# Filter ticks of a fused FFT convolution and spectral mix, moved from ticks 0 to 16 of the first pair to ticks 1 to 17

## The chip, the core and the metric

The kernel runs on one core of one Trainium2 chip. A core has TensorE (matmuls), VectorE and ScalarE (both read PSUM and copy or combine tiles), GpSimdE and SyncE; here the last two mostly issue DMAs. Each engine works through its own list of instructions in order, and semaphores hold an instruction until what it needs is there. The metric is the device time in microseconds (us) of one execution, as the median of several; less is better. The profile calls the engines PE, PEld (TensorE's weight loads), DVE, ACT, POOL and SP; SPq is SyncE's DMA queue.

## The reference: a causal convolution and a spectral mix

Two steps follow each other, on `x` of 8 x 5696 x 128 (batch, positions, channels):

```python
L = 2 * S
y = np.fft.irfft(np.fft.rfft(x, n=L, axis=1) * np.fft.rfft(h, n=L, axis=0)[None], n=L, axis=1)[:, :S]
x = y
X = np.fft.rfft(x, axis=1)                      # 64 lowest modes are mixed by w_r + i w_i
Yr = einsum("bmd,mde->bme", Xr, w_r) - einsum("bmd,mde->bme", Xi, w_i)
Yi = einsum("bmd,mde->bme", Xr, w_i) + einsum("bmd,mde->bme", Xi, w_r)
u = x + np.fft.irfft(Y, n=S, axis=1)
out = u + np.maximum(u @ w_ch, 0.0)
```

The long FFT is done as matrix products: 5696 is 89 x 64, a transform over the 89 is the first stage, one over the 64 with its twiddle factors the second, and the product with the transformed filter `h` stands between the way forward and the way back.

## The kernel before

**Pairs and ticks.** The eight batches are worked through as four pairs. A pair has 90 frequencies of the first stage, in 23 *ticks* of four (the last has two). The function `tick` (line 664) puts on record what belongs to one tick, engine by engine; each engine runs its list in the order of recording, and the recorder adds the waits (a write to a PSUM bank waits until the engines that read it are done). For tick t of the first pair it records, in this order:

- in ticks 3, 5, 7, 9, 11, 14, 17 and 20 a *placement* (`x_place`, line 364): VectorE copies a piece of the next pair's input from where it was loaded to `Xin`;
- the *second stage* of tick t (`second`, line 609): 16 matmuls of tile As with the strip M into two PSUM banks. `slot_of` (line 602) says which: banks 0 and 1 in the ticks that have a filter tick and in every odd tick, and 2 and 3 in even ticks without one;
- the *product* with the filter (`products`, line 629): ScalarE copies the two banks to a tile Xs (`copied`, line 589), and VectorE multiplies it with the filter's tiles Hs to U (line 652);
- the first step of the way back for tick t-2: four matmuls of U with Wc, ScalarE's two copies to Zs, and one DMA on SyncE that stores them to DRAM (`zscr<-Zs`);
- the *modes* of tick t-3: matmuls of G with Zs, summed in bank 7;
- a *filter tick* (`filter_tick`, line 490): the transform of `h` for one tick's frequencies.

Tick 0 is different: its second stage stands ahead of the loop but for its last eight columns, and its product is made of two pieces on VectorE (line 623), between which ScalarE copies bank 7 to Xs.

**The filter tick.** `filter_tick(f, banks)` makes 16 matmuls of Ah with M (eight in the last, f = 22), one copy of the two banks to Hs, and two DMAs on SyncE that put the same columns into the other half of Hs with the two halves of the partitions exchanged (`Hs<-Hs`). Product f needs the copy and both DMAs. For odd f up to 11 a DMA for a piece of the table G follows. The copy is made by ScalarE for f below 8 (but for f = 2) and by VectorE after that; the condition is in line 506. Filter ticks 0 to 5 stand among the first pair's first stage (tile As), and 6 to 22 in its ticks, always in banks 2 and 3. LH is 6, NT is 23, and the condition for a tick of the first pair to have one is in `with_h_at`, line 584:

```python
    def with_h_at(g_, t):
        return g_ == 0 and t + LH < NT
...
            return XSLOT[(t + 1) % 2 if not with_h_at(g_, t) else 0]
...
        if with_h:
            filter_tick(t + LH, [2, 3])
```

So filter tick t + 6 stands at the end of tick t, for t from 0 to 16. The eight semaphores of the ring for `Hs<-Hs` let four filter ticks be under way.

**Around the pair.** The first stage of the next pair (As) stands at the pair's end, copied by VectorE and ScalarE in turn. Later pairs have no filter ticks. The mix of the modes and the way back with the outputs follow after the four pairs.

Of the kernel before, what the change touches and what calls it, by code (L numbers as in the profile page):

```python
# [123 lines left out]
def bass_long_conv_fft__then__afno_spectral_mix_kernel(nc, x, h, moe_w_r, moe_w_i, moe_w_ch, out):  # L124
# [10 lines left out]
    NT = (NK + KT - 1) // KT  # L135
# [149 lines left out]
    def ap(t, row, p0, n, off, dims):  # L285
        return bass.AP(t, p0 * row + off, [[row, n]] + [list(d) for d in dims])
# [5 lines left out]
    def pv(bank, off, dims, p0=0, n=P):  # L292
        return bass.AP(ps, p0 * 4096 + bank * 512 + off, [[4096, n]] + [list(d) for d in dims])
# [5 lines left out]
    def bank(i):  # L299
        return ("bank", i)  # L300
# [3 lines left out]
    def evac(dst, src, reads, writes, scale=None, eng=None, after=()):  # L304
        e = eng
        if e is None:
            turn[0] ^= 1
            e = "scalar" if turn[0] else "vector"
        if e == "scalar":
            if scale is None:  # L310
                R.add(e, lambda h_: h_.copy(dst, src), reads, writes, after=after)  # L311
            else:
                R.add(e, lambda h_: h_.activation(dst, src, COPY, scale=scale), reads, writes, after=after)  # L313
        elif scale is None:
            R.add(e, lambda h_: h_.tensor_copy(dst, src), reads, writes, after=after)  # L315
        else:
            R.add(e, lambda h_: h_.tensor_scalar_mul(dst, src, scale), reads, writes, after=after)  # L317

    def dma(eng, dst, src, ring, reads=(), writes=(), after=()):
        R.add(eng, lambda h_: h_.dma_start(dst, src), reads, writes, ring=ring, after=after)  # L320

    def mm(o, l, r, st, sp, reads, writes):
        R.add("tensor", lambda h_: h_.matmul(o, l, r, start=st, stop=sp), reads, writes)  # L323
# [3 lines left out]
    def once(key, toks):  # L327
        if key in first:
            return []
        first[key] = 1  # L330
        return list(toks)
# [3 lines left out]
    def turns(name, items):  # L335
        i = ring2.get(name, 0)
        ring2[name] = i + 1
        return items[i % len(items)]
# [25 lines left out]
    def x_place(i, src, toks):  # L364
        R.add("vector", lambda e: e.tensor_copy(bass.AP(x_sb, i * XN * XS, [[XW, NQ], [XS, XN], [1, D]]),  # L365
                                                src),
              list(toks) + XZ, [("xin", i)])
# [51 lines left out]
    def mtok(k):  # L419
        t = [("m", k // KP)]  # L420
        if k % KP == KP - 1 and k < NK - 1:
            t.append(("m", k // KP + 1))
        return t
# [17 lines left out]
    for j in range(16):  # L441
        t = turns("h", [0, 2, 4])
# [7 lines left out]
        for i in range(LONG if j == 15 else 0):  # L450
# [5 lines left out]
             eng="vector" if j in (3, 7) else "scalar")  # L456
# [25 lines left out]
    def xtok(n):  # L482
        return [("xt", n, p_) for p_ in range(2)]

    def x_room(g_, i):
        if g_ > 1:
            return x_st[i]
        return x_h[i] if i < NXH else x_st[i - NXH]

    def filter_tick(t, banks):  # L490
        n = len(ticks[t])
        hb = banks
        for i, k in enumerate(ticks[t]):
            for r in range(2):
                for dh in range(2):
                    mm(pv(hb[dh], i * DH, [[1, DH]]),
                       ap(m_sb, MW, J * dh, J, k * 3 * J + (J if r == 0 else 0) + dh * J, [[1, P]]),
                       ap(ah_sb, HW, J * dh, J, (2 * k + r) * DH, [[1, DH]]), r == 0, r == 1,
                       AHT + mtok(k) + [("ag", k)], [bank(hb[dh])])
        lo, hi = KT * t * D, (KT * t + n) * D  # L500
        old = once("xr", [t_ for r_ in XR for t_ in r_]) if t == 0 else []
        for i in range(NXH):
            if KT * t + n > KH[i // 2]:
                old = old + once(("xh", i), xtok(i))
        evac(h_sb[:, lo:hi], pv(hb[0], 0, [[DH, n], [512, 2], [1, DH]]), [bank(hb[0]), bank(hb[1])], [("h", t, 0)],
             eng="scalar" if t < LH + 2 and t != 2 else "vector",
             after=old)
        for p0, p1 in ((0, J), (J, 0)):
            dma("sync", h_sb[p0:p0 + J, HW + lo:HW + hi], h_sb[p1:p1 + J, lo:hi], "s", [("h", t, 0)], [("h", t, 1, p0)])
        if t % 2 and t // 2 < NG:  # L510
            s0, s1 = t // 2 * GP, min(t // 2 * GP + GP, NS)
            dma("sync", g_sb[:, s0 * P:s1 * P], bass.AP(c_g, s0 * P, [[GW, P], [1, (s1 - s0) * P]]), "c", (),
                [("g", t // 2)], after=[("ag", k) for k in range(s0, s1)])
# [66 lines left out]
    LC, LM, LH = 2, 3, 6  # L580
# [1 line left out]
    XBANKS = [bank(0), bank(1), bank(2), bank(3)]  # L582

    def with_h_at(g_, t):
        return g_ == 0 and t + LH < NT

    onchip = {}

# [7 lines left out]
    def twin(g_, t):  # L596
        return g_ > 0 and t % 2 == 1

    def straight(g_, t):
        return g_ > 0 and t % 4 == 3  # L600
# [8 lines left out]
    def second(g_, t, d0=0, d1=D, bs=(0, 1)):  # L609
        sl = slot_of(g_, t)  # L610
        rd = AST if d1 == D else [("as", j) for j in range(d1 // 4)]
        for i, k in enumerate(ticks[t]):
            for r in range(2):
                for b in bs:
                    col = k * 3 * J + (J if r == 0 else 0) + b * J
                    mm(pv(sl + b, i * D + d0, [[1, d1 - d0]]),
                       ap(m_sb, MW, J * b, J, col, [[1, P]]),
                       ap(a_sb, AW, J * b, J, (2 * k + r) * D + d0, [[1, d1 - d0]]), r == 0, r == 1,
                       rd + mtok(k), [bank(sl + b)])
# [44 lines left out]
    def tick(g_, t):  # L664
        if g_ + 1 < NP:
            for i in range(2 * XC):
                if t == XPLACE[g_ > 0][i]:
                    x_place(i, bass.AP(x_room(g_ + 1, i), 0, [[XB, NQ], [D, XN], [1, D]]), xtok(i))
        with_h = with_h_at(g_, t)
        if t < NT:  # L670
            of_two = t > 0 and twin(g_, t - 1)
            if not of_two:
                if straight(g_, t):
                    second(g_, t + 1)
                if t:
                    second(g_, t)
                if t == 1:
                    d_ = DA if g_ else DF
                    second(g_, 0, d_, D, (0,))
                    first_u(0, (ps, slot_of(g_, 0) * 512), 4096, bank(slot_of(g_, 0)), d_, D)  # L680
            products(g_, t, slot_of(g_, t))
            if straight(g_, t):
                copied(g_, t + 1, slot_of(g_, t + 1))
            elif twin(g_, t):
                second(g_, t + 1)
        if g_ + 1 < NP:
            i = t // 2 - 1 if t % 2 == 0 else -1
            if g_ == 0:
                i = XLATE.index(t) + NXH if t in XLATE else -1
            if 0 <= i < 2 * XC:  # L690
                x_load(g_ + 1, i, x_room(g_ + 1, i), xtok(i), [("u", t % NU)] + AST)
        if LC <= t < NT + LC:
            s_ = t - LC
            n = len(ticks[s_])
            i, zi = s_ % NU, zroom(g_, s_)
            zb = [turns("z", ZBANK) for b in range(2)]
            for b in range(2):
                for r in range(2):
                    mm(pv(zb[b], 0, [[1, n * D]]), (W1, W2)[r], u_s[i][:, r * 1024 + b * 512:r * 1024 + b * 512 + n * D],
                       r == 0, r == 1, [("u", i), ("wc",)], [bank(zb[b])])  # L700
                evac(bass.AP(z_s[zi], b * D, [[1024, P], [2 * D, n], [1, D]]),
                     pv(zb[b], 0, [[D, n], [1, D]]), [bank(zb[b])], [("zs", zi, b)], eng="scalar",
                     after=once(("zx", zi, b), Z_OLD) if zi >= NZ else ())
                if b == 0:
                    drained(g_, t, 0)
            zo = (g_ * NK + KT * s_) * P * 256
            dma("sync", bass.AP(zs, zo, [[256, P], [P * 256, n], [1, 256]]),
                bass.AP(z_s[zi], 0, [[1024, P], [256, n], [1, 256]]), "z",
                [("zs", zi, 0), ("zs", zi, 1)], [("zd", g_, s_)])
        drained(g_, t, 1)  # L710
        late = g_ + 1 < NP and t in (NT, NT + 1)
        if late and t > NT:
            modes(g_, t - LM - 1)
            drained(g_, t, 2)
        if LM <= t < NT + LM and not (late and t == NT):
            modes(g_, t - LM)
        if with_h:
            filter_tick(t + LH, [2, 3])

    def drained(g_, t, at_):  # L720
        if g_ + 1 < NP:
# [244 lines left out]
```

## Time and profile before

| | |
|---|---|
| median of 3 runs | 372.16 us (371.73 to 372.21) |
| the profiled execution's own time | 371.89 us |
| its span, first to last instruction | 370.1 us |
| TensorE busy (share of the span), instructions | 354.7 us (96%), 5350 |
| VectorE | 291.8 us (79%), 332 |
| ScalarE | 316.2 us (85%), 499 |
| GpSimdE | 75.2 us (20%), 117 |
| granted TensorE clock, mean | 0.999 |
| DMA | 103.94 MB, mean 281 GB/s |

The page gives busy times of the engines and shares of the span. A line of the timeline has the start in us from the span's start, the time in us, the engine, the line of the kernel, the operation, and the tiles as out<-in with their shapes; what stands in brackets at the end is how long the engine was idle before it, and what it waited for. L311 and L315 are the copies of one helper (ScalarE and VectorE), L323 is the helper of all matmuls and L320 of all DMAs, so the tiles tell one use from another: `ps<-As,M` is the second stage, `ps<-Ah,M` a filter tick, `ps<-U,Wc` the way back, `ps<-G,Zs` the modes. The first pair's ticks run from about 42 to 88 us of the span. The chain of waits follows the work back from the last instruction to what released it. For DMAs a view by tile gives the time from issue to landing. A table by stretches of time gives the busy times, the granted clock and the share in which the DMA engines were busy (it can be a little over 1).

### The profile page before, as it was taken

Reading aid. Unit: us, or ns where it says so; the run is one execution under the profiler, and the core shown is the slowest. Engines: PE = TensorE matmul, PEld = TensorE weight load, DVE = VectorE, ACT = ScalarE, POOL = GpSimd, SP = SyncE. Lnnn points to the kernel's source line nnn. Section 1 sums busy time; section 2 is a strip of 40 time slices with the busy share of each in tenths; the row PEclk is TensorE's granted clock in tenths of the full one; section 3 lists DMA queues with packets and bytes.
Section 4 is the critical chain, followed back from the end, with each engine's and each line's share of the span. In section 5 each row is a group of like instructions: output and inputs, shape, how many; then the busy total and the mean of one; then the engine's idle time right before and its main releaser. Section 6 shows DMA issues by size and latency. Waiting matters only on the chain.

```text
span 370.1 us, 12455 instructions
## 1 busy us (share of the span) xinstructions
PE 354.7 (96%) x5350; PEld 276.5 (75%) x5350; DVE 291.8 (79%) x332; ACT 316.2 (85%) x499; POOL 75.2 (20%) x117
## 2 busy tenths in 40 slices
PE   7999899999999999999999999999999999999994
PEld 7878766667866668866668766668899888888873
DVE  3549899988999999989999988775357777756666
ACT  8559999999999999999999999995467777688885
POOL 8804012100833311823213001151000000000000
PEclk9999999999999999999999999999999999999999
DMA  7999979969999996999996999999999999999878
GB/s 139 209 271 382 249 165 292 232 198 283 93 140 213 263 258 186 132 160 215 263 278 128 171 310 363 342 345 388 381 410 386 413 410 408 418 399 376 326 291 349
DMA packets 87048, 103.94 MB, mean 281 GB/s; under 512 B 22730, under 2 KB 72522, under 8 KB 83438
## 3 DMA queue, kind: packets, MB, share of 16 engines
q1 hardware_dynamic: 64610, 81.33, 62.5%
q0 software_dynamic: 22384, 21.83, 35.4%
q8 instruction: 42, 0.69, 0.7%
q14 instruction: 12, 0.10, 0.1%
HBM read 70.61 MB, written 51.12 MB: 329 GB/s over the span
## 4 chain that ended last, share of the span: by engine, by line
PE 78%; ACT 10%; DMA 7%; DVE 3%; issue 1%; POOL 1%; DVEq 0%; POOLq 0%
PE ps L323 78%; ACT As L313 6%; DMA out_dram<-O 5%; DMA Hin<-in_h_dram 2%; ACT R L898 1%; DVE As L317 1%; ACT Xs L311 1%; DVE U L623 1%; POOL Hin L320 1%; ACT UT L311 1%; DVE O L899 0%; ACT Zs L311 0%; DVE Hp L438 0%; ACT C L313 0%; DVE Hs L315 0%
## 5 line engine op out<-in xcount | busy, mean ns | idle before, releaser
L652 DVE TENSOR_TENSOR U<-Xs,Hs 128x2048 f16<-128x2048 f16 (+1 forms) x72 | 85.8, 1197 | 12.1 <-ACT Xs L311 11.5
L323 PE MATMUL ps<-U,Wc 128*128 128x512 f16 (+1 forms) x368 | 93.8, 376 | 1.4 <-DVE U L623 1.4
L311 ACT CAST Xs<-ps 128x1024 f16<-128x1024 f32 (+1 forms) x76 | 75.0, 995 | 5.8 <-PE ps L323 3.1
L311 ACT CAST Zs<-ps 128x512 f16<-128x512 f32 (+1 forms) x132 | 70.1, 605 | 0.7
L899 DVE TENSOR_TENSOR O<-ps,R 128x512 f32<-128x512 f32 x81 | 52.4, 684 | 21.6 <-ACT R L898 11.4
L898 ACT ACTIVATE R<-ps 128x512 f32<-128x512 f32 (+1 forms) x92 | 50.5, 592 | 8.5 <-PE ps L323 8.4
L317 DVE TENSOR_SCALAR As<-ps 128x720 f16<-128x720 f32 x64 | 53.1, 879 | 4.8 <-PE ps L323 3.3
L323 PE MATMUL ps<-As,M 64*128 64x128 f16 (+3 forms) x1504 | 52.5, 214 | 2.4 <-ACT As L313 1.2
L313 ACT ACTIVATE As<-ps 128x720 f16<-128x720 f32 (+1 forms) x68 | 48.2, 771 | 5.0 <-PE ps L323 4.8
L323 PE MATMUL ps<-F,Xin 128*128 128x180 f16 x512 | 52.1, 249 | 0.1
L323 PE MATMUL ps<-WI,UT 128*128 128x256 f16 x360 | 50.8, 278 | 0.5 <-ACT UT L311 0.4
L311 ACT CAST UT<-ps 128x712 f16<-128x712 f32 x46 | 34.5, 752 | 19.4 <-PE ps L323 18.4
L323 PEld LDWEIGHTS ps<-U,Wc 128*128 128x128 f16 x368 | 29.1, 97 | 28.2 <-DVE U L623 1.9
L323 PEld LDWEIGHTS ps<-F,Xin 128*128 128x128 f16 x512 | 45.2, 155 | 6.7 <-DVE Xin L365 0.9
L323 PEld LDWEIGHTS ps<-As,M 64*128 64x128 f16 x1504 | 42.2, 94 | 8.7 <-ACT Xs L311 1.9
L323 PEld LDWEIGHTS ps<-WI,UT 128*128 128x128 f16 x360 | 38.9, 152 | 3.2 <-issue 1.8
L323 PE MATMUL ps<-IBs,C 128*128 128x356 f16 x128 | 39.2, 314 | 0.8 <-DVE O L899 0.7
L320 POOL DMA_DIRECT2D Xt<-in_x_dram x40 | 21.4, 540 | 76.5 <-PE ps L323 76.0
L323 PEld LDWEIGHTS ps<-G,Zs 128*128 128x128 f16 x512 | 26.1, 96 | 14.1 <-ACT Zs L311 0.2
L652 DVE TENSOR_TENSOR U<-ps,Hs 128x2048 f16<-128x2048 f32 (+1 forms) x16 | 35.5, 2216 | 0.0
L323 PE MATMUL ps<-G,Zs 128*128 128x128 f16 (+2 forms) x512 | 31.9, 192 | 0.1
L311 ACT CAST Zt<-ps 128x512 f16<-128x512 f32 x52 | 29.1, 659 | 0.0
(76 smaller groups left out, 479.4 us busy)
## 6 DMA issues: line engine op xcount, KB each, us to landing
out_dram<-O SPq DMA_DIRECT2D x39, 512.0 KB, 10.5
zscr<-Zs SPq DMA_DIRECT2D x62, 256.0 KB, 6.7
zscr<-Zt SPq DMA_DIRECT2D x26, 256.0 KB, 6.6
Xt<-in_x_dram POOLq DMA_DIRECT2D x20, 320.0 KB, 6.9
W<-wscr SPq DMA_DIRECT2D x4, 1024.0 KB, 8.5
ZT0a<-zscr SPq DMA_DIRECT2D x4, 1024.0 KB, 11.0
M<-cM POOLq DMA_DIRECT2D x5, 720.0 KB, 17.6
ZT1a<-zscr SPq DMA_DIRECT2D x3, 1024.0 KB, 11.1
```

The costliest lines, as they stand in the source:

```text
L311: R.add(e, lambda h_: h_.copy(dst, src), reads, writes, after=after)
L313: R.add(e, lambda h_: h_.activation(dst, src, COPY, scale=scale), reads, writes, after=after)
L317: R.add(e, lambda h_: h_.tensor_scalar_mul(dst, src, scale), reads, writes, after=after)
L320: R.add(eng, lambda h_: h_.dma_start(dst, src), reads, writes, ring=ring, after=after)
L323: R.add("tensor", lambda h_: h_.matmul(o, l, r, start=st, stop=sp), reads, writes)
L623: R.add("vector", lambda e: e.tensor_tensor(bass.AP(u_s[0], b * 512 + d0, [[2048, P], [1024, 2], [D, n], [1, d1 - d0]]), bass.AP(s_[0], s_ ...
L652: R.add("vector", lambda e: e.tensor_tensor(uv, src, hv, MULT), bk + [("h", t, 0), ("h", t, 1, 0), ("h", t, 1, J)], [("u", i)])
L898: R.add("scalar", lambda e: e.activation(rv, src_r, RELU), bk, [("r", i % NR)], after=once(("r", i % NR), G_ALL + XTT + [("y", 0), ("y", 1 ...
L899: R.add("vector", lambda e: e.tensor_tensor(ov, src_u, rv, ADD), bk + [("r", i % NR)], [key + (h_,)], after=once(key, old))
```

## The change

The condition for a filter tick in the first pair becomes `0 < t < NT - LH + 1`, that is ticks 1 to 17, and tick t has filter tick t + 5 in place of t + 6. Filter ticks 6 to 22 each stand one tick later, with their copies, their two DMAs and, for 7, 9 and 11, the DMA of a piece of G. The condition for ScalarE copies goes from f below 8 to f below 7, so of the filter ticks in the pair only number 6 is copied by ScalarE and number 7 by VectorE. `slot_of` uses the same condition; for tick 17 it gives banks 0 and 1 either way, so the second stage's banks are the same in every tick.

```diff
         evac(h_sb[:, lo:hi], pv(hb[0], 0, [[DH, n], [512, 2], [1, DH]]), [bank(hb[0]), bank(hb[1])], [("h", t, 0)],
-             eng="scalar" if t < LH + 2 and t != 2 else "vector",
+             eng="scalar" if t < LH + 1 and t != 2 else "vector",
              after=old)
...
     def with_h_at(g_, t):
-        return g_ == 0 and t + LH < NT
+        return g_ == 0 and 0 < t < NT - LH + 1
...
         if with_h:
-            filter_tick(t + LH, [2, 3])
+            filter_tick(t + LH - 1, [2, 3])
```

In the list of SyncE the order around the pair's start becomes Hs 6, z 0, Hs 7, G 3, z 1, Hs 8, where it was Hs 6, Hs 7, G 3, z 0, Hs 8, z 1 (Hs f are the two DMAs of filter tick f, z t the store of tick t's Zs). On TensorE filter tick 22 stands directly ahead of the second stage of tick 18, where it stood ahead of that of tick 17.

## The prediction on record

> **What bounds the kernel now.** I read the page first, then the chain of waits in order of time, then the timeline of the first pair (42 to 90 us), then the tile view of Hs for its transfers. The page's chain is TensorE for most of the span:
>
> ```profile
> PE 78%; ACT 10%; DMA 7%; DVE 3%; issue 1%; POOL 1%; DVEq 0%; POOLq 0%
> ```
>
> The chain in order of time (start, us, what) shows where the first pair hangs:
>
> ```profile
> 43.67 0.58 ACT Xs L311
> 44.26 0.49 ACT Hs L311
> 44.75 0.93 ACT Xs L311
> ...
> 45.72 3.61 PE ps L323 x63
> ...
> 74.60 20.63 PE ps L323 x300
> ...
> 95.26 7.47 ACT As L313 x11
> ```
>
> Two things are to be seen. In tick 0 the ScalarE copy of filter tick 6 (Hs, 0.49 us) stands between two Xs copies, and TensorE waits for the second of these before tick 2 (0.47 us idle at 45.72, by the timeline). From there to 95 us TensorE is the chain, so what delays it in ticks 2 to 22 comes through whole. With a filter tick in it a tick takes 2.08 us (70.36 to 72.44), without one 1.85 (78.64 to 80.49). ScalarE is as full: 10.00 us of the 10 from 80 to 90.
>
> The timeline around the last filter tick, number 22, which now stands in tick 16 (start, us, engine, line, what):
>
> ```profile
> 75.59 0.68 DVE L315 CAST Hs<-ps 128x512 f16<-128x512 f32 x1
> ...
> 76.54 1.22 DVE L652 TENSOR_TENSOR U<-Xs,Hs 128x2048 f16<-128x2048 f16 x1 [0.26 <-ACT Xs L311]
> ...
> 76.68 0.29 PE L323 MATMUL ps<-Ah,M 64*128 64x64 f16 x8
> ...
> 77.68 0.41 DVE L315 CAST Hs<-ps 128x256 f16<-128x256 f32 x1
> ...
> 78.02 0.68 DVE L365 COPY Xin<-Xt 89x2048 f16<-89x2048 f16 x1
> ...
> 78.62 1.21 DVE L652 TENSOR_TENSOR U<-Xs,Hs 128x2048 f16<-128x2048 f16 x1
> 78.64 0.62 PE L323 MATMUL ps<-As,M 64*128 64x128 f16 x16
> ...
> 80.49 0.62 PE L323 MATMUL ps<-As,M 64*128 64x128 f16 x16
> ```
>
> The eight Ah matmuls (76.68) are filter tick 22, in banks 2 and 3. Behind them comes the second stage of tick 17 (76.81), which writes banks 0 and 1; that of tick 18 (78.64) is the first to write 2 and 3 again. VectorE has emptied them by 78.09, so nothing waits. VectorE does a placement (Xin), product 17 and a copy in this order.
>
> SyncE's queue issues without a break from 46.65 to 78.5 us, and each half of Hs that it moves for filters 8 to 18 lands 3.7 to 6.5 us after its issue:
>
> ```profile
> 64.86 0.59 SPq L320 DMA_DIRECT2D zscr<-Zs  x1
> 65.55 1.14 SPq L320 DMA_DIRECT2D Hs<-Hs  x2
> 66.73 0.59 SPq L320 DMA_DIRECT2D zscr<-Zs  x1
> ```
>
> The tile view for the second of the two at 65.55 alone (it is issued at 66.1):
>
> ```profile
> DMA to landing us min/median/max: 6.5/6.5/6.5
> ```
>
> That is filter 14's half: it lands at 72.6, and product 14 starts at 72.72. Worked out in the same way, 13 is there 0.3 us ahead of its product, 15 0.8, 16 0.3, 17 0.5, and 8 to 12 1.8 to 2.4. The margin with which the filter arrives is nearly used up.
>
> **The change, part by part.** *1. Tick 0 loses filter tick 6 (minus 0.47).* Its matmuls (16, about 0.23 us of TensorE in a row of them) leave a place where TensorE waits anyway. Its copy leaves ScalarE, so the Xs copy of tick 1 starts when the one before it lets it, at 44.16 in place of 44.63. Tick 2 then starts 0.47 us earlier. What is late next: product 2 on VectorE, now at 47.42, would start at 46.95; product 1 ends at 46.92 and Hs half 2 landed at 46.8, so both just allow it. Filter tick 6 takes the place that 7 had in tick 1, with the same ScalarE copy; 7 goes to tick 2 and VectorE, where 8 stood. So ticks 1 to 15 keep their number of instructions on each engine.
>
> *2. Tick 18 must wait for filter tick 22 (plus 1.85).* Tick 16 now gets the full filter tick 21 and tick 17 the half one, 22. The matmuls of 22 are directly followed by the second stage of tick 18, in the same banks 2 and 3, and it waits until VectorE has copied 22; behind it on TensorE stand the matmuls of U and G of that tick, and for these ScalarE's copies. VectorE's order after product 16 is copy 21, placement, product 17, copy 22. From the start of product 16 by starts of the same forms: 1.14 (76.54 to 77.68), 0.60 for a full copy (71.36 to 71.96), 0.60 for the placement (78.02 to 78.62), 1.14 for product 17, 0.41 for the copy and 0.06 to TensorE (a copy ended at 74.54 and released 74.60): 3.95. 76.54 + 3.95 = 80.49, against 78.64: 1.85 later. The larger filter tick in 16 and the added one in 17 cost TensorE 0.23 together (2.08 less 1.85), which lies inside this wait. It is not got back: from 78.64 to 87 TensorE and ScalarE are both full, and the chain goes on over both at 95.26.
>
> *3. The filter's transfers are later in SyncE's queue (plus 1.15).* Each Hs pair moves behind one more store of Z: the order was Hs 8, z 1, Hs 9; it becomes z 1, Hs 8, z 2. A z issue takes 0.68 us to the next one (mean of the seven from 50.31 to 64.86). As the queue has no idle time, Hs 8 to 17 are issued 0.68 later, not a tick later, and the products want them 0.47 earlier: 1.15 off margins of 0.1 to 0.8 us. Product 14 is the first that gives way far: 72.72 + 0.68. It then holds VectorE, the copy behind it, and by bank 2 and 3 the next filter tick (74.60, which already waits 0.18 for a copy). So the head start is gone and TensorE is 0.68 late when step 2 comes. Bounds of this shift: zero, if the z stores fill time in which the DMA engines idle (share 0.49 from 48 to 50, 0.61 from 50 to 52) and the landing comes no later, and then the head start stays; above, 1.5 us, the share that 256 of 384 KB have in a SyncE cycle of about 2.3 us (60.95 to 74.61 is six). I take 0.68, the nearest row, since the time from issue to landing hardly changes over those rows.
>
> The Trainium skill bears on this ("DMA: Bandwidth & Descriptors", "Queues, rings and completion order"): each DMA engine consumes descriptors in ring order. By that rule a pair behind a z also waits for its data; 256 KB at the 246 GB/s of 60 to 70 us is 1.07, and the sum would be 0.39 higher than mine. The trace's DMA share (1.06 there, full) agrees with it, that of 48 to 52 doesn't yet bite.
>
> *Sum:* minus 0.47 plus 1.85 plus 1.15 = plus 2.53. The profiled execution took 371.89 us (span 370.1): 374.4. It lies 0.27 below the median of the runs shown (372.16), so runs may centre at 374.7.
>
> Costs set at nothing: the other moved issues on SyncE (cG pieces 3, 4, 5 come a tick later; each is read first at least ten ticks after its issue), the VectorE copy in place of a ScalarE one (VectorE gains it in tick 17, where it is counted), the placements and the loads of the next pair (they keep their ticks).
>
> **Rivals.**
> *A. The filter lands in time.* Steps 1 and 2 alone: plus 1.38, 373.3. For it: idle DMA early, z stores sooner. Against: five of the margins lie under 1.15. Chance 0.27.
> *B. Tick 18 doesn't wait,* as VectorE has copied 22 when TensorE arrives: minus 0.47 plus 0.23, 371.65, not slower. It decides at 78.4 us; copy 22 would have to be ready 2 us before VectorE's row of forms allows, with product 17 and a placement ahead of it. If the order of banks is not what I read from the code, it is this case too. Chance 0.04.
> *C. The clock falls in the wait.* TensorE would come to tick 18 at 78.64 + 0.23 + 0.68 = 79.55 and go on at 80.49 + 0.68 = 81.17, so it stands still for 1.6 us; in 42 to 45 us it was idle 0.7 of 3 us in pieces up to 0.5, and the granted clock stayed 1.00; no row has a longer gap after the start. At half clock a tick of 1.85 costs as much again: about 376.3. The skill's "TensorE: Matmul & The Clock Gate" (Part 1) says a window of about 3.4 us without work halves it; that gap is shorter. Chance 0.03.
> *D. Transfers are later than 0.68,* up to 1.5: 375.2; it is the upper end of my forecast's own range.
>
> **How the numbers follow.** Forecast with D's part 0.62, A 0.27, B 0.04, C 0.03, the rest (something unseen on either side) 0.04. The forecast's range is 373.9 to 375.5 (with the median's 0.27). A is likely enough that the range takes it in: 373.1 to 375.6. About 0.2% (0.74 us) is what a measurement of this kernel can tell from no change: faster than 371.4 has 0.02, between 0.05 (B and a little), slower 0.93.
>
> **What would show it.** Step 1: the second stage of tick 2 near 45.25, and no Hs copy between two Xs copies at 44. Step 2: a TensorE wait of 1.4 to 2 us for VectorE Hs ahead of an As x16 near 80 to 81, which the trace of before hasn't. Step 3: products 13 to 17 starting right at a landing, with VectorE idle ahead of them, and TensorE waiting for Hs copies near 75. If TensorE runs through at 79 the prediction is wrong; if it waits there but products 13 to 17 start 0.47 earlier than now, A holds.

## The result, and the profile after

The changed kernel takes 376.56 us in the median of 13 runs (374.16 to 380.66), before 372.16 in the 13 runs beside it; the ratio is 1.010 with a 95% interval of 1.0063 to 1.0137. It is 4.4 us slower by the medians, where 2.5 were forecast. Its profiled execution took 374.27 us (span 372.5), only 2.38 above that of before: it is one of the quick ones. Two repeats in later runs gave 1.0079 (1.0054 to 1.0105) and 1.0120 (1.0084 to 1.0156).

Page of the changed kernel, the chain by engine:

```profile
PE 63%; DMA 14%; ACT 9%; DVE 7%; issue 3%; POOL 2%; SPq 1%; DVEq 0%; POOLq 0%
```

The chain of waits of the changed kernel from 43 to 95 us, in order of time:

```profile
46.10 1.02 ACT Xs L311
...
60.09 6.03 DMA Hs<-Hs
...
73.40 5.63 DMA Hs<-Hs
...
81.15 0.42 DVE Hs L315
81.57 0.05 issue
81.62 13.45 PE ps L323 x186
```

Before, TensorE was the chain from 45.72 to 95 us. Now it has 36% of the chain in this stretch; transfers of the filter have 22%, VectorE's filter copies 13%, and VectorE's products and placements stand between them. The Hs copy ahead of the Xs copy at 46.10 is gone. The same stretch as waits (engine waited for what, us in all, times, longest):

```profile
PEld ps L323 <- DVE Hs L315: 3.8, 6, 1.6
...
PE ps L323 <- DVE Hs L315: 2.8, 5, 1.4
DVE U L652 <- DMA Hs<-Hs: 1.2, 1, 1.2
```

The second stage of tick 2, in the profile before and in the one after (which is 0.21 us late from tick 0 on, 43.03 against 42.82):

```profile
45.72 0.62 PE L323 MATMUL ps<-As,M 64*128 64x128 f16 x16 [0.47 <-ACT Xs L311]
```

```profile
45.44 0.62 PE L323 MATMUL ps<-As,M 64*128 64x128 f16 x16
```

And the timeline where tick 18 follows filter tick 22:

```profile
79.41 0.68 DVE L365 COPY Xin<-Xt 89x2048 f16<-89x2048 f16 x1
...
79.89 0.29 PE L323 MATMUL ps<-Ah,M 64*128 64x64 f16 x8
80.01 1.22 DVE L652 TENSOR_TENSOR U<-Xs,Hs 128x2048 f16<-128x2048 f16 x1
...
81.15 0.41 DVE L315 CAST Hs<-ps 128x256 f16<-128x256 f32 x1
...
81.62 0.62 PE L323 MATMUL ps<-As,M 64*128 64x128 f16 x16 [1.44 <-DVE Hs L315]
```

This is step 2 as it was forecast: the eight matmuls of filter tick 22, then placement, product 17 and copy 22 on VectorE, and TensorE waiting for that copy. What this profile doesn't show is the other 2 us of the median. They stand in executions with a lower mean clock. Of the 24 executions of the changed kernel that the comparisons used (12 and two times 6), 14 have a mean granted clock of 0.995 or less, with a median of 377.0 us; the other 10 have 375.0. Of 129 executions of before that later runs list with their clocks, 5 are that low. Six executions more than 1.5% above the fastest of their kernel are left out of these counts and of the ratios as disturbed (one of the changed kernel, three of before, one each of e12 and e18), and all six are that low too.

What 0.995 stands for can be read from the 20 profiles. Six of them have one fall to half clock after the clock first rose and before 360 us, and means of 0.991 to 0.995; the other 14 have none, and 0.996 to 0.999. (All 20 have half clock at the very end too, which is what brings a mean without a fall down to 0.996.)

### The profile page after: what moved, and what is told of

It is laid out like the page before. It is cut to its first block, busy times and chain, and to the rows that moved or that the text cites. A ratio compares the mean times of both kernels' runs of the same rounds, so it can differ in the third digit from the quotient of the medians.

```text
span 372.5 us, 12453 instructions
## 1 busy us (share of the span) xinstructions
PE 354.0 (95%) x5350; PEld 275.6 (74%) x5350; DVE 292.6 (79%) x333; ACT 316.1 (85%) x498; POOL 74.9 (20%) x117
## 4 chain that ended last, share of the span: by engine, by line
PE 63%; DMA 14%; ACT 9%; DVE 7%; issue 3%; POOL 2%; SPq 1%; DVEq 0%; POOLq 0%
PE ps L323 63%; ACT As L313 6%; DMA out_dram<-O 4%; DMA Xt<-in_x_dram 4%; DMA Hs<-Hs 3%; DMA Xr<-in_x_dram 3%; DVE Hs L315 2%; ACT R L898 1%; DVE Xin L365 1%; DVE As L317 1%; DVE U L652 1%; DVE U L623 1%; POOL Hin L320 1%; ACT Xs L311 1%; SPq L320 1%
## 5 line engine op out<-in xcount | busy, mean ns | idle before, releaser
L311 ACT CAST Zs<-ps 128x512 f16<-128x512 f32 (+1 forms) x132 | 70.1, 602 | 1.3 <-PE ps L323 0.8
```

## The experiments

Times are medians. Ratios are to the kernel before on the same chip, with 95% intervals. "Low" counts executions with a mean clock of 0.995 or less.

### The changed kernel again (e1, e16)

No edit.

> The changed kernel again, unaltered. Its 13 runs so far have a median 4.4 us above the median of before, its profiled execution only 2.4 us, with mean granted clocks from 0.989 to 0.999. Theory W (waits): only the waits of the prediction count, tick 18's for VectorE (1.4 to 1.6 us in the profile) and a late Hs transfer (0.8 to 1.2 us); then the time is 2 to 3 us above before, in runs of equal clock. Theory C (clock): the waits also let the granted clock fall in most executions; then runs with a clock of 0.993 are 2 to 3 us above runs with 0.998, and the runs of before on the same chip keep about 0.999.

Measured: 375.84 us, 1.0079; low 3 of 6, with a median 1.1 us above that of the other three (theory C said 2 to 3). This profile caught a low execution. Stretches of 3.41 us (from:to, us, busy time of PE and so on, granted clock behind POOL):

```profile
80.08:83.49 3.41, 1.54 (x24) 0.88 (x24) 2.91 (x5) 1.96 (x3) 0.00 (x0) 1.00 0.80 236
83.49:86.90 3.41, 3.41 (x34) 1.91 (x34) 1.22 (x1) 2.13 (x3) 0.00 (x0) 0.50 0.70 203
```

The wait in tick 18 is 1.9 us here (81.52 to 83.39), as product 17 itself starts late, right behind a landing (81.69 and 81.77). It lies whole in the first of the two stretches and leaves TensorE busy for 1.54 of 3.41 us, and in the next 3.41 us the granted clock is one half.

> The changed kernel a third time. Theory C: about half of the executions with a clock of 0.995 or less, and these 1 to 2.5 us above the others; median 375.5 to 376.5. The profile shows the wait in tick 18 of 1.4 to 2 us and waits of products for Hs transfers of 1 to 3 us in all.

Measured: 376.67 us, 1.0120; low 3 of 6 (376.98 to 378.72 us, the others 374.20 to 376.36). The profile has the wait of 1.4 us and one of 1.7 for a transfer.

### Without the wait in tick 18 (e2), without the change in SyncE's order (e3), without either (e4)

```diff
-            filter_tick(t + LH - 1, [2, 3])
+            filter_tick(t + LH - 1, [0, 1] if t == NT - LH else [2, 3])
```

> The changed kernel with filter tick 22 (in tick 17) in banks 0 and 1, which are free there, so that tick 18's second stage in banks 2 and 3 needs no copy of VectorE. Theory W: 1.4 to 1.6 us less than the changed kernel, some 1 us above before; the wait for the Hs transfer stays. If that wait in tick 18 is what costs clock (theory C), the granted clock goes back to that of before as well and the time falls by 3 us or more. If the prediction's step 2 is wrong, no difference from the changed kernel.

Measured: 373.61 us, 1.0029 (1.0009 to 1.0048), low 3 of 12. 2.2 us less than e1 on the same chip: more than the wait alone, less than theory C's 3. The second stage of tick 18 starts 0.12 us behind the start of filter tick 22:

```profile
80.88 0.29 PE L323 MATMUL ps<-Ah,M 64*128 64x64 f16 x8
81.00 0.61 PE L323 MATMUL ps<-As,M 64*128 64x128 f16 x16
```

For e3 the store is recorded behind the filter tick:

```diff
-            dma("sync", ... zs ..., "z", ...)
+            def store(): dma("sync", ... zs ..., "z", ...)
+            if not with_h: store()
...
             filter_tick(t + LH - 1, [2, 3])
+            if t >= LC: store()
```

> The changed kernel with the store of Z in a tick recorded behind the filter tick, so that SyncE's list is that of before, instruction for instruction. Theory W: no product waits for an Hs transfer before tick 17, 0.6 to 1.2 us less than the changed kernel; the wait of 1.4 to 1.9 us in tick 18 stays and the head start of 0.47 is kept, so 1.2 to 1.6 us above before. Rival: the transfers land late whatever the order, as they start a tick later; then no difference from the changed kernel.

Measured: 375.76 us, 1.0078 (1.0052 to 1.0105), low 5 of 10: no difference from the changed kernel. The rival of this expectation fits: products 10, 12 and 16 still start right at a landing (0.08 us behind it). SyncE's list is that of before, but each pair of DMAs waits for a copy that is made a tick later, and what is behind it waits too: filter 8 is issued at 52.02, before at 50.87.

> Both together: filter tick 22 in banks 0 and 1, and the store of Z behind the filter tick. Theory W: no wait of the changed kernel is left and the head start of 0.47 us stays, less 0.23 for TensorE in ticks 16 and 17: 0.2 us under before, which can hardly be told from no change. Theory C: the same if the clock follows the waits; if the clock falls for another reason (a chip, the first tick), this kernel has the low clock too and stays 2 us above before.

Measured: 373.73 us, 1.0025 (1.0004 to 1.0046), low 0 of 12. As e2, and not the 0.2 us under before that theory W forecast: the order brings nothing here either, and some 1 us (1.5 by the median) is left that isn't the wait in tick 18.

### The wait by itself (e5) and filled with matmuls (e6)

```diff
-            filter_tick(t + LH, [2, 3])
+            filter_tick(t + LH, [0, 1] if t == NT - LH - 1 else [2, 3])
```

> The kernel before with one thing altered: filter tick 22 (in tick 16) in banks 0 and 1, so that the second stage of tick 17 right behind it must wait for VectorE's copy. It has the wait of the changed kernel without anything else of the change. Theory W: by the trace of before the copy ends at 78.09 and the second stage would have started at 76.81, so 1.3 us more than before, not more. Theory C: the wait is shorter than that of the changed kernel (1.4 to 2.0 us), so fewer of its executions lose clock; a window of 3.41 us with 1.3 us of wait is busy for 0.61 of it, and windows with 0.57 to 0.61 kept the clock in the traces so far, one with 0.45 lost it: clock as in before, 0.996 to 0.999.

Measured: 373.25 us, 1.0036 (1.0002 to 1.0069), low 3 of 12; 1.1 us above before, where 1.3 was expected. The clock wasn't that of before as expected: the three low executions are 375.34 to 376.92 us. In the profile the wait is 1.7 us and products 10, 13 and 16 start right at a landing, so this is not the wait of 1.3 us by itself.

```diff
             filter_tick(t + LH - 1, [2, 3])
+            for i in range(18 if t == NT - LH else 0):
+                mm(pv(6, 0, [[1, 2 * NK]]), f1_sb[:, 0:P], f1_sb[:, :], True, True, [("f1",)], [bank(6)])
```

> The changed kernel with 18 matmuls of 180 columns into bank 6, whose result nobody reads, between filter tick 22 and the second stage of tick 18 (about 1.4 us): they fill most of TensorE's wait and don't change what it waits for. Theory C: no window of TensorE is then mostly idle, the clock stays at 0.996 or more in all executions, and the time is that of the changed kernel's runs with full clock, 374.5 to 375, 1 to 1.5 us less than its median. Theory W (waits alone cost, the clock figure is a symptom): the same time as the changed kernel or a little more, 376 to 376.5.

Measured: 375.94 us, 1.0100 (1.006 to 1.014), low 2 of 6. By its time this is what theory W forecast, not theory C. But the fill isn't where it was meant to be: in the profile filter tick 22 itself waited 1.66 us for copy 21, as product 16 was late, and the fill stood behind that wait. So it doesn't decide; e13 and e14 do.

### Step 1 by itself (e7, e15) and step 3 by itself (e8)

Filter tick 6 of the kernel before loses its matmuls and copy:

```diff
-        for i, k in enumerate(ticks[t]):
+        for i, k in enumerate(ticks[t] if t != LH else []):
...
+        if t == LH: R.add("gpsimd", lambda e: e.memset(h_sb[:, lo:hi].bitcast(U32), 0), (), [("h", t, 0)], ...)
+        else: evac(h_sb[:, lo:hi], ...)
```

> The kernel before without the matmuls and the copy of filter tick 6 in tick 0; GpSimdE fills its columns of Hs with zeros instead, so four frequencies of the result are left out, and all DMAs stay as they are. It is the change's step 1 by itself. Prediction: tick 2 starts 0.47 us earlier; where the Hs transfers leave room, the time is 0.5 us under before. Rival: the transfers' margin of 0.1 to 0.8 us in products 13 to 17 is used up by the earlier ticks, and nothing or only 0.1 to 0.2 us is gained.

> The kernel of e7 again: before without filter tick 6's matmuls and copy in tick 0, GpSimdE filling its columns with zeros, so four frequencies are left out. Prediction's step 1: 0.5 us under before. What e7 said: 1.0042, 1.5 us above. If the transfers of Hs give back what the head start gains, it lies at no change, 0.999 to 1.002; if it is above 1.002 again, the head start itself costs, and the step is wrong in sign.

Measured: 373.56 us, 1.0042 (1.0018 to 1.0066), and again 372.99, 1.0035 (1.0012 to 1.0058). The head start alone costs 1.1 to 1.4 us, which neither the step nor its rival forecast. The earlier start is there (in e7 the second stage of tick 2 starts at 45.46, 0.47 earlier once the 0.2 us by which this execution started later is taken off), and is more than lost in waits for transfers: product 13 waits 1.6 us in e7 and 2.5 in e15, and product 15 starts right at a landing in both. From the waits of e15, 40 to 95 us (L654 is the line of the products, 652 before the edit added two lines):

```profile
DVE U L654 <- DMA Hs<-Hs: 2.5, 1, 2.5
```

An earlier start can use up a margin; it doesn't say why the halves of filter 13 land at 71.3 and 72.0, where they landed by 69.9 in the first profile of before. That stays open.

For e8 the kernel before records the DMAs of a filter tick in the next tick, behind the store of Z:

```diff
-        for p0, p1 in ((0, J), (J, 0)): dma("sync", h_sb[...], h_sb[...], "s", ...)
+        def moves(): ...            # the same DMAs
+        if t < LH: moves()
+        else: pend.append(moves)    # done in the next tick, behind dma("sync", ... zs ..., "z", ...)
```

> The kernel before with only SyncE's list altered: the DMAs of a filter tick (and of G) are recorded one tick later, behind that tick's store of Z, which makes SyncE's list that of the changed kernel, instruction for instruction. Engines' lists stay those of before. It is step 3 by itself. If the late transfers cost what the changed kernel without the wait in tick 18 costs, 1.0 to 1.3 us above before (ratio 1.003), with products 10 to 17 starting right at a landing. Rival: the copies' later place is what makes them late, not SyncE's order; then less than 0.4 us.

Measured: 373.38 us, 1.0041 (1.0016 to 1.0067): 1.2 us, as step 3 said (1.15). Products 8, 10, 13 and 16 start right at a landing.

### The kernel before once more (e9) and another queue for the stores (e10, e11, e12)

> The kernel before, unaltered, against itself: what a ratio of no change looks like, and a second profile of it. Ratio 1.000 with an interval of 0.002 to 0.004 on either side. The prediction read from one profile that no product waits for an Hs transfer in it (margins 0.08 to 0.8 us for filters 13 to 17). If this profile shows such waits of 0.5 to 1.5 us, the kernel before stands at the edge itself, and its spread of 370.5 to 375 us comes from there; if not, the spread has another cause.

Measured: 1.0012 (0.9991 to 1.0033). The second profile of before, of the slowest of these 12 executions, isn't like the first:

```profile
DVE U L652 <- DMA Hs<-Hs: 2.6, 1, 2.6
```

```profile
71.17:74.58 3.41, 1.66 (x37) 1.02 (x38) 2.39 (x4) 2.76 (x5) 0.00 (x0) 1.00 1.05 210
74.58:77.99 3.41, 3.41 (x46) 1.92 (x42) 2.26 (x4) 2.34 (x4) 0.00 (x0) 0.50 0.97 293
```

The second half of filter 13 lands at 72.1 here, at 69.9 in the first profile; product 13 waits 2.6 us, a window falls below half, and the clock halves. So the kernel before has both troubles in some executions. The stores of Z land late too: ScalarE waits 2.0 us for one before it can write its Zs tile, and TensorE is idle for 1.10 us of this window behind that, for 0.66 behind the copy that follows product 13.

```profile
71.82 1.07 ACT L311 CAST Zs<-ps 128x512 f16<-128x512 f32 x2 [2.02 <-DMA zscr<-Zs]
```

```profile
72.46 0.61 PE L323 MATMUL ps<-U,Wc 128*128 128x512 f16 x2 [1.10 <-ACT Zs L311]
...
74.08 0.41 PE L323 MATMUL ps<-Ah,M 64*128 64x64 f16 x16 [0.66 <-DVE Hs L315]
```

```diff
-            dma("sync", bass.AP(zs, ...), ..., "z", ...)
+            dma("gpsimd" if g_ == 0 else "sync", bass.AP(zs, ...), ..., "z" if g_ else "q", ...)
```

> The kernel before with the stores of Z of the first pair issued by GpSimdE in place of SyncE, so that SyncE issues only Hs and G there. If SyncE's rate of issue makes the Hs transfers late, they are issued right after their copies and land several us ahead of their products; the time is that of the quiet executions of before, 371 to 372, with a smaller spread. If the DMA engines themselves are the limit, the landings stay where they are and the time doesn't fall.

Measured: 372.28 us, 1.0012 (0.9987 to 1.0037): no gain, and no smaller spread (371.00 to 374.58). In the profile, which is of the slowest of the 12 executions, SyncE issues filter 13 at 60.7 in place of 63.1, and its two halves land at 70.1 and 71.2, in place of 67.2 and 69.9. The tile view of Hs for the first of the two:

```profile
DMA to landing us min/median/max: 9.3/9.3/9.3
```

> The changed kernel with filter tick 22 in banks 0 and 1 and with the stores of Z of the first pair on GpSimdE: both of the change's losses taken away. If the two are all there is, the head start of 0.47 us less 0.23 in ticks 16 and 17 is left: 0.2 us under the kernel before with the same stores (e10), which can't be told from it. If step 1 brings nothing even then, it lies above e10.

Measured: 371.66 us, 1.0006 (0.9978 to 1.0035), low 1 of 12. Both losses are gone; it can't be told from before. With the stores on SyncE the same kernel (e2) took 373.61 us. The profile is of the quickest of its 12 executions: no product waits for a transfer, and filter 13, issued at 61.8, has landed by 68.0, 2.0 us ahead of its product. Its chain is TensorE again from 51 to 95 us:

```profile
51.45 43.58 PE ps L323 x798
```

> The changed kernel with the stores of Z of the first pair on GpSimdE, and nothing else altered: the wait in tick 18 stays, the late transfers go. Theory W: the wait alone, 1.6 to 1.9 us above the same with banks 0 and 1 (e11). Theory C: executions in which the clock falls behind tick 18 (0.993) are 1 to 2 us above those in which it doesn't; with the other waits gone the window around tick 18 is busy for more than half, so they are fewer than in the changed kernel, where 8 of 12 had it.

Measured: 373.39 us, 1.0035 (1.0009 to 1.0062). The wait in tick 18 is worth 1.7 us here (373.39 less 371.66; the intervals of the two ratios overlap), where the forecast had 1.85. One low execution of 11. With the stores on SyncE the same kernel had 14 of 24 and a time 2.5 to 3.3 us longer (ratios 1.0079 to 1.0120). The window around tick 18 in its profile, and the next:

```profile
77.41:80.82 3.41, 1.71 (x30) 1.03 (x30) 2.98 (x5) 1.97 (x3) 1.50 (x2) 1.00 0.74 255
80.82:84.23 3.41, 3.41 (x54) 2.07 (x48) 1.23 (x2) 3.00 (x5) 0.72 (x1) 1.00 0.31 110
```

1.71 of 3.41 us is 0.502: a hair over half, and the clock stays. This profile is of the one low execution all the same: its clock falls elsewhere, far from the change:

```profile
265.14:268.55 3.41, 1.45 (x25) 1.22 (x26) 0.23 (x1) 0.40 (x1) 0.00 (x0) 1.00 1.09 365
268.55:271.96 3.41, 3.41 (x39) 2.82 (x36) 0.67 (x1) 1.15 (x2) 0.00 (x0) 0.50 0.97 375
```

### The clock apart from the wait (e13, e14)

e13 is e12 with product 17 recorded twice; e14 adds matmuls that nobody reads.

```diff
+            if t == NT - LH:
+                products(g_, t, slot_of(g_, t))
             filter_tick(t + LH - 1, [2, 3])
+            for i in range(36 if t == NT - LH else 0):        # e14 only
+                mm(pv(6, 0, [[1, 2 * NK]]), f1_sb[:, 0:P], f1_sb[:, :], True, True, [("f1",)], [bank(6)])
```

> The kernel of e12 (the change, stores of Z of the first pair on GpSimdE) with product 17 made twice by VectorE, which writes the same values again and makes tick 18 wait 1.14 us longer, about 2.8 us in all. In the traces so far every window of 3.41 us in which TensorE was busy for less than half was followed by 3.41 us of half clock, and no window above half was. A wait of 2.8 us falls below half in one window unless it is split nearly evenly over two. Theory C: most executions have a clock of 0.995 or less, and the time is 1.1 us (the wait) plus about 1.2 us (the clock, by ticks 18 to 20 of e1) above e12: 375.5 to 376. Theory W: 1.1 us above e12, 374.5, whatever the clock.

> The same longer wait as e13, filled with 36 matmuls of 180 columns into bank 6 whose result nobody reads (2.8 us). Theory C: the clock stays at 0.996 or more in nearly all executions, and the time is that of e12 plus the wait, 374.5, 1 us or more under e13. Theory W: the same as e13.

Measured: e13 376.18 us, 1.0101 (1.0071 to 1.0130), low 6 of 6; e14 374.77 us, 1.0075 (1.0044 to 1.0107), low 0 of 8. TensorE's timeline of e13, then of e14:

```profile
81.30 0.62 PE L323 MATMUL ps<-As,M 64*128 64x128 f16 x16 [2.75 <-DVE Hs L315]
...
83.74 1.04 PE L323 MATMUL ps<-As,M 64*128 64x128 f16 x16
...
86.51 0.62 PE L323 MATMUL ps<-As,M 64*128 64x128 f16 x16
```

```profile
78.36 2.96 PE L323 MATMUL ps<-F 128*128 128x180 f16 x36
81.26 0.62 PE L323 MATMUL ps<-As,M 64*128 64x128 f16 x16
...
83.11 0.62 PE L323 MATMUL ps<-As,M 64*128 64x128 f16 x16
...
84.95 0.62 PE L323 MATMUL ps<-As,M 64*128 64x128 f16 x16
```

Tick 18 starts at the same time in both. Two ticks then take 5.21 us in e13 and 3.69 in e14. The granted clock of e13 in two windows around it:

```profile
78.95:82.36 3.41, 1.06 (x19) 0.73 (x20) 2.26 (x3) 0.52 (x2) 0.75 (x1) 1.00 0.58 197
82.36:85.77 3.41, 3.41 (x30) 1.86 (x29) 1.23 (x1) 2.55 (x4) 0.75 (x1) 0.50 0.17 54
```

Theory C holds for the clock: the same wait, filled, doesn't cost it. A fall costs 1.5 us (5.21 less 3.69) in the two profiles. The medians differ by 1.4 (376.18 less 374.77), but the intervals of the two ratios overlap.

### Later loads (e17, e18)

```diff
-    XLATE = [3, 6, 9, 12]
+    XLATE = [5, 9, 12, 15]
```

> The kernel before with the four loads of the next pair's input that stand in ticks 3, 6, 9 and 12 moved to ticks 5, 9, 12 and 15 (356 KB each); their placements stay in 11, 14, 17 and 20. If the DMA engines' load is what makes Hs late, fewer bytes lie ahead of Hs 8 to 15, no product of 13 to 17 waits for one, and the time is 0.3 to 1 us under before (ratio 0.997 to 0.999). If these loads have nothing to do with it, ratio 1.000 within 0.002, with the same waits.

> The changed kernel with filter tick 22 in banks 0 and 1 and the same four loads in ticks 5, 9, 12 and 15. If the loads are what makes Hs late, the 1 us that e2 lay above before goes, and what is left of the change is its head start: 0 to 0.5 us under before. If not, it stays at 1.003.

Measured: e17 373.10 us, 1.0026 (1.0002 to 1.0049); e18 374.24 us, 1.0048 (1.0023 to 1.0074). Nothing is gained, and e17 is even a little slower than either forecast; in e18's profile one product waits 3.9 us for a transfer. So these loads two or three ticks later don't help. Whether the load of the DMA engines as a whole makes the transfers late isn't decided by this: from 54 to 78 us their busy share in stretches of 4 us is 0.85 to 1.13 in the first profile of before and 1.00 to 1.11 in that of the changed kernel.

## Why the prediction was wrong

**Step 1, minus 0.47: the head start is there, but by itself it costs.** Tick 2 starts at 45.44 in the changed kernel, 0.49 earlier once its 0.21 us later start is taken off. Alone (e7, e15) it makes the kernel 1.1 to 1.4 us slower; it costs nothing that can be told where the stores of Z are on another queue (e11). The prediction counted a wait for transfers only under step 3; it belongs here just as well.

**Step 2, plus 1.85: right.** The wait is where it was put, 1.4 us in the first profile and 1.9 in the second, where 1.6 were worked out under C; taking it away gives 1.7 us (e12 less e11) where the stores are on another queue.

**Step 3, plus 1.15: size about right, working not.** e8 measured 1.2, and e2 and e4, which keep it and the head start, lie 0.9 to 1.1 us above before by their ratios (1.4 and 1.5 by the medians). But the shift of issue is not 0.68 for each: filters 8 to 16 are issued 0.9 to 1.8 us later than before (filter 8 at 52.27 in place of 50.87, filter 13 at 64.67 in place of 63.13), of which 0.21 is the later start. The landings don't move by the same: filter 10 lands 3.3 us later and filter 14 not at all. The first product to wait was 10, by 1.2 us, not 14. The margins were read from a single execution; e9 shows that they differ by 2 us between executions of the same kernel. Why the transfers land so late is open in part. The changed kernel is rid of most of the loss when the stores of Z leave SyncE (e11 beside e2, e12 beside e1 and e16), so what SyncE is given to issue has a part in it; but the order of its list alone isn't it (e3, e4), the kernel before gains nothing by the same step (e10), and later loads don't help (e17).

**The sum's number is that of executions with full clock:** plus 2.53 from 371.89, or 374.7 by the median; the ten of them have 375.0. Part of this is luck, as one of its three terms had the wrong sign by itself and another came about in another way.

**The step that failed is rival C, "the clock falls in the wait",** to which the prediction gave 0.03 and which it kept out of the sum and the range. 14 of 24 executions have such a fall, and their median is 2.0 us longer (377.0 less 375.0); a single fall is 1.5 of that by e13 and e14, and the rest can be second falls (clocks of 0.989) and the longer waits themselves. The price put on it was 1.85 and the time 376.3, near the 376.56 measured; that is luck too, as the median lies between executions with and without a fall. What was wrong is the reason against it: that 1.6 us of standing still is shorter than a window without work. The runs show that a window need not be empty, only less than half busy. The row that the prediction leaned on, 0.7 us idle of 3 with the clock at 1.00, is far from half and couldn't tell the two apart.

The wait in tick 18 doesn't do it alone. The 1.44 us of the first profile by themselves leave a window busy for 0.58 at the least (an estimate: 1 less 1.44/3.41), and with the stores on another queue, where the wait stays, one of 11 executions is low, and that one by a fall elsewhere (e12). In e1 a late transfer holds product 17 by 0.34 us and stretches the wait to 1.9 us; without these 0.34 the window would have been busy for 0.55 (an estimate: 1.54 and 0.34 of 3.41), and with them it is 0.45. Without the wait but with the late transfers, 3 of 24 are low (e2, e4). So in most cases it takes both, and how the windows lie then decides. Of the changed kernel's low executions one alone was profiled (e1); that the fall stands behind tick 18 in the others as well is inferred from these counts.

## What to carry to other kernels

When work is moved to a later place, look at which PSUM banks the next writer of its new place uses: a step that was free one tick earlier can stand directly ahead of a writer of its own banks. A margin of a few tenths of a microsecond for a DMA, read from one execution, is no margin; profile the kernel twice before leaning on it. A stall of TensorE of more than half a clock window can have a second price in the ticks behind it, as can shorter stalls close together. If it can't be removed, matmuls of no use in it keep the clock (e13, e14: a stall of 2.75 us), provided that they stand in the stall and not behind another one (e6). Before a cause is left out of a sum as too small, look for a row that could have shown it.

## What the runs showed of the hardware that was not expected

In all the traces here the clock changes at whole windows of 3.41 us, counted from when it first rises: in e1 it rises at 8.39 and falls at 83.49, 75.10 us or 22.0 windows later. Counting windows between the first rise and 360 us in the 20 traces, every window in which TensorE's matmuls took at most 0.486 of the time (six: 0.15, 0.27, 0.31, 0.43, 0.45, 0.49) was followed by one at half clock, and every window of 0.502 and more by one at full clock; the half clock lasted for one window. The Trainium skill ("TensorE: Matmul & The Clock Gate", Part 1) has the same free-running window and asks for a whole idle one before the clock falls; the traces agree on the window, and on the idle share the measurement decides.

A DMA of 64 KB within SBUF that stood in a busy queue landed 9.3 us after its issue in e10, where the same one issued 2.4 us later landed 4.0 us after it in the first profile of before, and 6.0 us after it in e11 (issued at 61.8). So an early issue brought an early landing in one execution and not in another, and what tells them apart isn't shown.
